# bf16 casts ahead of bf16 TensorE transposes, and DMA-cast MoE output weights, in a fused Longformer-attention and MoE kernel

## The chip, the cores and the metric

One core of one Trainium2 chip. Times are device microseconds (us) of that core; each run is one launch. In the views PE is TensorE and PEld its weight loads, DVE is VectorE, ACT ScalarE, POOL GpSimd and SP SyncE; a q after the name (SPq) is the engine's queue, which issues transfers. Those of SyncE go out on what the profile calls a hardware queue, those of GpSimd on a software queue; the core's 16 DMA engines carry both.

## The reference

```python
# q, k, v: [8 batches, 8 heads, 576 rows, 64]; global_idx: 8 sorted row numbers
scores = (1 / sqrt(64)) * q @ k.T
mask = (abs(i - j) <= 32) | i in global_idx | j in global_idx
attn = softmax(where(mask, scores, -1e9))
x = (attn @ v).transpose(0, 2, 1, 3).reshape(4608, 512)
h = x @ w_in                      # [512, 2048]
r = maximum(h, 0.0)
out = (s * r * r + b) @ w_out     # [2048, 512]; s and b are scalars
```

## The kernel before

A batch has four pairs of heads, a pair eight steps. Each step holds one block of scores, exponentials or products with v, and one "quantum" (a quarter of a row block) of the MoE of an earlier batch. Rows of q and k are cut in five blocks of 128, with 8 slots for the global rows in each (in q at row 60, in k and v at row 0). They are loaded as rows and transposed on TensorE; a transfer called the fill puts the global rows of a batch into their slots.

```python
natk = [const.tile([P, NCH, H, D], FP32, ...) for i in range(2)]   # natq the same
...
def load_q(eng, bi, h0, nh, part):          # 60 rows a block, two parts; load_k: 120 rows
    ...
    for c in range(NCH):
        a = KC * c + HB * part
        n = min(HB, S - a)
        r = (HB + NG) * part
        eng.dma_start(out=d[r : r + n, c, h0 : h0 + nh],
                      in_=q[bi, h0 : h0 + nh, a : a + n].rearrange("h s d -> s h d"))
...
def load_v(bi):                             # fp32 in DRAM, bf16 tile: cast by the DMA
    ... nc.gpsimd.dma_start(out=d[NG : NG + n, c, :, 0:D], in_=v[...])
...
def fill(bi):                               # the global rows of a batch, from DRAM scratch
    for d, src, r in ((natk[bi % 2], gsk, 0), (natq[bi % 2], gsq, HB), (vbufs[bi % 2], gsv, 0)):
        ... nc.sync.dma_start(...)
def prefetch_hw(bi):
    load_k(nc.sync, bi, 0, H)
    load_q(nc.sync, bi, 0, H, 0)
    load_q(nc.sync, bi, 0, H, 1)
    fill(bi)
...
def trans_a(p):                             # fp32 transposes, eviction casts to bf16
    ps = ps_s.tile([P, 512], FP32, tag="s", name="pst")
    for c in range(4):
        tr(ps, P * c, natk[bi % 2], c, hp)
    ...
    nc.scalar.copy(out=kt[:, 0:512], in_=ps[:])
...
for p in range(4, 4 * B):                   # the loop from batch 1 on
    ...
    if hp == 1 and bi + 1 < B:
        load_v(bi + 1)
        prefetch_hw(bi + 1)
    run_pair(p, nq, p + 1 < 4 * B)          # transposes of pair p + 1 at steps 5 and 6
```

The sum of the rows of `w_out`, which the bias needs, is added up on VectorE while ScalarE casts the weights (`weights_out`).

The softmax here doesn't subtract the row's maximum and nothing guards it: scores larger than these inputs give would overflow.

## Time and profile before

| | before |
|---|---|
| median of 3 runs | 438.07 us (436.57 to 438.22) |
| profiled span | 436.0 us |
| first score product of batches 0 to 7 | 20.2, 96.2, 124.0, 165.5, 207.0, 248.4, 289.8, 331.2 us |
| one batch, from batch 2 on | 41.4 to 41.5 us |
| PE busy over the whole span | 387.0 us |
| first MoE product | 72.7 us |

A batch's length is the distance between the first score products of two batches in the trace. The two things to keep in mind for what follows: from batch 2 on PE is the bound (busy 38.6 to 38.7 of every 40 us from 160 to 320 us), and k of the next batch is issued at 256.21 us but first read by a transpose at 285.08 us, 28.9 us later:

```profile
285.08 0.60 PE L349 MATMUL pst<-identf,natk 128*128 128x128 f32 x4
```

(The timeline of PE before: start, length, engine, line, operation, output from inputs.)

### The profile page before, as it was taken

Reading aid. Unit: us, or ns where it says so; the run is one execution under the profiler, and the core shown is the slowest. Engines: PE = TensorE matmul, PEld = TensorE weight load, DVE = VectorE, ACT = ScalarE, POOL = GpSimd, SP = SyncE. Lnnn points to the kernel's source line nnn. Section 1 sums busy time; section 2 is a strip of 40 time slices with the busy share of each in tenths; the row PEclk is TensorE's granted clock in tenths of the full one; section 3 lists DMA queues with packets and bytes.
Section 4 is the critical chain, followed back from the end, with each engine's and each line's share of the span. In section 5 each row is a group of like instructions: output and inputs, shape, how many; then the busy total and the mean of one; then the engine's idle time right before and its main releaser. Section 6 shows DMA issues by size and latency. Waiting matters only on the chain.

```text
span 436.0 us, 8254 instructions
## 1 busy us (share of the span) xinstructions
PE 387.0 (89%) x3063; PEld 241.8 (55%) x3063; DVE 265.6 (61%) x650; ACT 206.7 (47%) x405; POOL 84.5 (19%) x162
## 2 busy tenths in 40 slices
PE   1686984869799999999999999999999999999996
PEld 1563761325455655775577568656755665554442
DVE  7817443597776766676677567666766775442432
ACT  1013321855556733763476447645754673360530
POOL 9744932005005001300310050005000100100000
PEclk9999999989999999999999999999999999999999
DMA  8999194499519911991396169419941000101001
GB/s 134 154 229 257 13 147 58 170 193 97 55 48 151 150 46 67 157 143 52 88 147 111 50 122 148 75 57 138 140 86 50 26 0 30 71 2 65 31 26 72
DMA packets 128367, 42.00 MB, mean 96 GB/s; under 512 B 118655, under 2 KB 120703, under 8 KB 128327
## 3 DMA queue, kind: packets, MB, share of 16 engines
q1 hardware_dynamic: 83724, 34.00, 40.7%
q0 software_dynamic: 43328, 7.16, 24.1%
q8 instruction: 24, 0.39, 0.4%
q10 hardware_dynamic: 1275, 0.31, 0.4%
q14 instruction: 16, 0.13, 0.1%
HBM read 38.82 MB, written 9.83 MB: 112 GB/s over the span
## 4 chain that ended last, share of the span: by engine, by line
issue 49%; PE 30%; POOL 10%; ACT 5%; DVE 4%; POOLq 1%; DMA 1%; ACTq 0%; DVEq 0%
PE psh L518 10%; PE pso L533 10%; POOL vx L170 4%; POOL xt L498 3%; PE psg L391 3%; PE po L450 3%; PE pst L349 2%; ACT e L427 1%; ACT r L525 1%; PE pss L423 1%; DMA wo<-in_moe_w_out_dram 1%; POOL vx L124 1%; ACT kt L363 1%; POOLq L206 1%; DVE vx L417 1%
## 5 line engine op out<-in xcount | busy, mean ns | idle before, releaser
L518 PE MATMUL psh<-xt,win_t 128*128 128x512 bf16 (+7 forms) x1024 | 145.5, 289 | 15.8 <-POOL xt L498 12.3
L533 PE MATMUL pso<-wout_t,g 128*128 128x512 bf16 x576 | 141.1, 379 | 0.0
L525 ACT ACTIVATE r<-psh 128x512 bf16<-128x512 f32 x144 | 89.5, 627 | 80.7 <-PE psh L518 77.8
L427 ACT ACTIVATE e<-pss 128x384 bf16<-128x384 f32 (+1 forms) x160 | 75.5, 484 | 106.6 <-PE pss L423 105.4
L518 PEld LDWEIGHTS <-win_t 128*128 128x128 bf16 x1024 | 86.8, 98 | 62.6 <-issue 21.3
L528 DVE TENSOR_TENSOR g<-r 128x512 bf16<-128x512 bf16 x144 | 60.6, 424 | 53.8 <-ACT r L525 51.8
L533 PEld LDWEIGHTS <-g 128*128 128x128 bf16 x576 | 55.3, 98 | 55.9
L430 DVE TENSOR_TENSOR em<-e,mask 128x384 bf16<-128x384 bf16 (+1 forms) x160 | 54.6, 342 | 36.8 <-ACT e L427 35.5
L498 POOL COPY xt<-xg 128x4 bf16 x72 | 15.7, 218 | 271.9 <-DVE xg L496 239.1
L423 PE MATMUL pss<-qbd,kt 128*128 128x384 bf16 (+1 forms) x160 | 51.4, 337 | 12.1 <-POOL qbd L302 4.0
L542 DVE SCALAR_TENSOR_TENSOR osb<-pso,s_bc,bias_row 128x512 f32<-128x512 f32 x36 | 26.9, 747 | 31.8 <-PE pso L533 31.8
L381 DVE CAST qbd<-pst 64x512 bf16<-64x512 f32 x64 | 44.1, 689 | 2.1 <-PE pst L349 1.2
L450 PE MATMUL po<-em,vx 128*64 128x160 bf16 (+3 forms) x896 | 37.1, 233 | 3.1 <-DVE vx L417 1.7
L450 PEld LDWEIGHTS <-vx 128*64 128x64 bf16 x896 | 29.7, 117 | 14.5 <-issue 7.9
L349 PE MATMUL pst<-identf,natk 128*128 128x128 f32 x160 | 30.0, 295 | 8.7 <-DMA natk<-in_k_dram 8.6
L170 POOL DMA_DIRECT2D vx<-in_v_dram x40 | 35.3, 897 | 3.2 <-issue 3.2
L349 PE MATMUL pst<-identf,natq 128*128 128x128 f32 x160 | 28.8, 298 | 5.7 <-ACT kt L363 4.8
L349 PEld LDWEIGHTS pst<-identf,natk 128*128 128x128 f32 x160 | 20.9, 150 | 18.7 <-POOL identf masks.py:199 8.6
L481 DVE TENSOR_TENSOR xt<-po,rep 128x600 bf16<-128x600 f32 x32 | 25.1, 783 | 8.6 <-ACT rep L479 8.6
L423 PEld LDWEIGHTS <-kt 128*128 128x128 bf16 x160 | 15.5, 100 | 25.8 <-DVE qbd L381 6.1
L363 ACT CAST kt<-pst 128x512 bf16<-128x512 f32 x32 | 20.1, 629 | 18.2 <-PE pst L349 18.2
L349 PEld LDWEIGHTS pst<-identf,natq 128*128 128x128 f32 x160 | 19.7, 150 | 11.6 <-ACT kt L363 9.1
(75 smaller groups left out, 202.0 us busy)
## 6 DMA issues: line engine op xcount, KB each, us to landing
out_dram<-osb SPq DMA_DIRECT2D x36, 256.0 KB
natq<-in_q_dram SPq DMA_DIRECT2D x63, 120.0 KB
natk<-in_k_dram SPq DMA_DIRECT2D x28, 240.0 KB
wo<-in_moe_w_out_dram SPq DMA_DIRECT2D x4, 1024.0 KB
vx<-in_v_dram POOLq DMA_DIRECT2D x32, 120.0 KB, 8.4
win_t<-in_moe_w_in_dram POOLq DMA_DIRECT2D x4, 512.0 KB, 15.5
natk<-in_k_dram SPq DMA_DIRECT2D x7, 192.0 KB
natk<-in_k_dram SPq DMA_DIRECT2D x8, 120.0 KB
```

The lines of the kernel that those rows point to most:

```text
L170: nc.gpsimd.dma_start(out=d[NG : NG + n, c, :, 0:D], in_=v[bi, :, KC * c : KC * c + n].rearrange("h s d -> s h d"),)
L349: nc.tensor.transpose(ps[:, dst0 : dst0 + P], src2(src)[:, c, P * hp : P * hp + P], identf[:])
L381: nc.vector.tensor_copy(out=qdst(p, hh, 0, 512), in_=ps[r])
L423: nc.tensor.matmul(ps[:], ktile[p][:, P * c : P * c + P], qbufs[p % 3][:, :, LO[c] : HI[c]])
L427: nc.scalar.activation(e[:], ps[:], AF.Exp, scale=SCALE)
L430: later.append(lambda: nc.vector.tensor_mul(em[:], e[:], masks[c][:]))
L450: nc.tensor.matmul(po[D * hh : D * hh + D, a : a + n], vx[:, c, 2 * hp + hh, D * part : D * part + D], emt[(p, c)][:, hh, x : x + n], star ...
L498: nc.gpsimd.tensor_copy(out=xt[:, :, ds(greg_p[i], 1)], in_=xg[:, :, i : i + 1])
L518: nc.tensor.matmul(psh[:, d0 : d0 + n], win_t[:, a, f * P : f * P + P], xts[bi][:, a, x0 : x0 + n], start=(a == 0 and j == 0), stop=(a == ...
L525: nc.scalar.activation(r[:], psh[:], AF.Relu)
L528: later.append(lambda g=g, r=r: nc.vector.tensor_mul(g[:], r[:], r[:]))
L533: nc.tensor.matmul(pso[:], gl[f][:, u * P : u * P + P], wout_t[:, f], start=(f == 0), stop=(f == 15),)
```

## The change

Its intent: transposes in bf16 instead of fp32, twice as fast and evicted in fewer copies; `w_out` cast by the software queue's DMA instead of ScalarE, as `w_in` already was, and its row sum taken by accumulating transfers; the one-hot selection of global rows in the first two batches instead of the first alone, the rest taken from the DRAM scratch as before. To get bf16 rows, ScalarE casts k and q and GpSimd casts v, one batch ahead, from one fp32 tile for each. Core of the diff:

```diff
-    natk = [const.tile([P, NCH, H, D], FP32, ...) for i in range(2)]
-    natq = [const.tile([P, NCH, H, D], FP32, ...) for i in range(2)]
+    nat = {t: const.tile([P, NCH, H, D], FP32, ...) for t in "kqv"}
 ...
     def load_q(eng, bi, h0, nh, part):
         for c in range(NCH):
-            a = KC * c + HB * part
-            n = min(HB, S - a)
+            a = KC * c + (HB - NG) * part
+            n = min(HB + NG * part, S - a)          # the second part: 68 rows
 ...
-    def load_v(bi):                                  # GpSimd queue, casting
+    # load_kv(nc.gpsimd, "v", ...): GpSimd queue, fp32 to fp32; cast later by GpSimd
 ...
+    def cast(eng, t, bi, h0, nh):
+        hs = slice(h0, h0 + nh)
+        dst = vbufs[bi % 2][:, :, hs, 0:D] if t == "v" else cast_t[(t, bi)][:, :, hs]
+        eng(out=dst, in_=nat[t][:, :, hs])
 ...
-            nc.tensor.transpose(ps[...], src2(src)[:, c, ...], identf[:])      # fp32
+            nc.tensor.transpose(ps[...], src2(cast_t[(t, bi)])[:, c, ...], ident[:])  # bf16
 ...
+    def casts_for(bi):                               # third and fourth pair of a batch
+        return ({1: [cast k half 0 on ACT], 4: [cast q half 0 on ACT], 5: [cast v half 0 on POOL]},
+                {1: [cast k half 1 on ACT], 4: [cast q half 1 on ACT], 5: [cast v half 1 on POOL]})
+    def fetch(bi, fills):
+        load_batch(bi, 0, H)                         # k, q part 0, q part 1 on the sync queue
+        load_kv(nc.gpsimd, "v", bi, 0, H)
+        for t in fills:
+            fill(t, bi)
 ...
+    def wsum_part(j):                                # in batch 1: sum of w_out by DMA
+        if j == 0:
+            nc.sync.dma_start(out=wsum[:], in_=w_out2[:, 0:4])
+        else:
+            nc.gpsimd.dma_start(out=wsum[:], in_=w_out2[:, 4*j : 4*j+4], accum_op=OP.add)
 ...
         if hp == 1 and bi + 1 < B:
-            load_v(bi + 1)
-            prefetch_hw(bi + 1)
+            new_casts(bi + 1)
+            fetch(bi + 1, "kqv")
+        if hp >= 2 and bi + 1 < B:
+            ex = casts_for(bi + 1)[hp - 2]
```

(The bodies of `casts_for` are abbreviated here: each entry is a step of the pair and what is cast in it. The line `# load_kv ...` is a note and stands for code.)

## The prediction

> **What bounds the kernel now.** I read the engine table, the busy table by stretches of time, the groups by shape, the time line of one late batch, and the sync queue's time line, in that order.
>
> ```profile
> PE 387.0 (89%) x3063; PEld 241.8 (55%) x3063; DVE 265.6 (61%) x650; ACT 206.7 (47%) x405; POOL 84.5 (19%) x162
> ```
> ```profile
> 80.00:90.00 10.00, 6.57 (x30) 2.72 (x28) 7.11 (x15) 8.18 (x13) 0.00 (x0) 1.00 0.85 256
> ...
> 240.00:280.00 40.00, 38.67 (x358) 27.55 (x357) 27.74 (x69) 22.98 (x47) 6.01 (x13) 1.00 0.80 108
> ```
> ```profile
> L349 PE MATMUL pst<-identf,natk 128*128 128x128 f32 x160 | 30.0, 295 | 8.7 <-DMA natk<-in_k_dram 8.6
> L381 DVE CAST qbd<-pst 64x512 bf16<-64x512 f32 x64 | 44.1, 689 | 2.1 <-PE pst L349 1.2
> L378 DVE CAST qbd<-pst 64x128 bf16<-64x128 f32 x64 | 18.2, 284 | 0.4
> L391 PE MATMUL psg<-selq,natq 128*128 128x8 f32 x40 | 9.1, 361 | 0.0
> L600 ACT CAST wout_t<-wo 128x2048 bf16<-128x2048 f32 x4 | 7.6, 1905 | 0.3 <-DMA wo<-in_moe_w_out_dram 0.3
> ```
>
> The columns after a stretch are its length and the busy time of PE, PEld, DVE, ACT, POOL, then clock, DMA share, GB/s. From about 125 us on, PE is busy 38.7 of 40 us: it is the bound. Before that, waits bound: 80 to 90 us is 6.6 us of PE behind the output-weight casts.
>
> ```profile
> 256.46 0.20 POOL xt L498
> ...
> 297.86 0.21 POOL xt L498
> ```
> ```profile
> 265.86 0.14 PEld L349 LDWEIGHTS pst<-identf,natq 128*128 128x128 f32 x1
> ...
> 266.41 0.42 PEld L349 LDWEIGHTS pst<-identf,natq 128*128 128x128 f32 x4 [0.40 <-ACT kt L363]
> ...
> 266.80 0.86 PEld L518 LDWEIGHTS <-win_t 128*128 128x128 bf16 x8
> ```
> ```profile
> 256.21 4.32 SPq L150 DMA_DIRECT2D natk<-in_k_dram  x5
> 260.62 13.44 SPq L161 DMA_DIRECT2D natq<-in_q_dram  x10
> 274.10 0.47 SPq L324 DMA_DIRECT2D natk<-gsk  x1
> ```
>
> The chain of waits repeats every 41.4 us: one batch, four head pairs of eight steps, each step with a quarter of a MoE row block. In a pair the transposes take PE from 264.44 to 264.88 and from 265.75 to 266.80, 1.49 us, of which 0.4 wait for the ACT eviction. The sync queue needs 18 us to issue one batch of k and q loads; the global rows (the fill) come last, at 274.1, and stream until about 279 in the trace's packets. Nobody waits for that here: the tiles are double, and the first transpose of the batch comes later.
>
> [...]the trace has no bf16 transpose, its fp32 ones take 105 to 110 ns each in the run above. [...]From 256 to 279 us the trace's hardware queue has 247 four-byte semaphore packets, beside the 16 of one store: 60 and 120 rows on 15 engines, 96 on 16, 36 on 12, 8 on 8 (76+75+72+24=247).[...]
>
> **The change, part by part.** *Transposes:* ten at an estimated 56 ns are 0.56 us in place of 1.49, so 0.93 a pair, 3.7 a batch. The new block phase also hides the 1 us that the first product after POOL's row copies waits each batch. PE alone would need 41.4-4.7, about 37 us a batch, 1.16 a step.
>
> *DVE:* before, a pair has 2x689+2x284+283 = 2.2 us of evictions; after, three copies of 640 elements, 1.5 us at 2x or 2.5 at 1x. DVE has 27.7 of 40, so neither binds.
>
> *ACT:* loses 0.63 a pair (k eviction), gains four casts of 128x1280 a batch: at 1905/2048 = 0.93 ns an element 1.2 us each, 5 a batch. They fall in the third and fourth pair. The third has eight Relus (5.0), five Exps (2.4), Ln and reciprocal (1.5) and two casts (2.5): 11.4 us against PE's 9.3. Some 2 us a batch come back, even with data ready: 39.
>
> *Start:* fp32 selects cost 4.07 us a pair on the chain; in bf16, ten small matmuls are under 1 us. Three pairs after the first go from 11.4 to about 9, 6.5 and 6.5. DVE's added memsets and the first casts set the first score product at about 24 us instead of 20.2. First MoE product: 63 instead of 72.7. Block before batch 1: 14 quanta in 72.7 to 96.5 become 11 quanta and the first transposes in some 14 us, to 77; the ACT weight casts, the 1 MB waits and 11 DVE additions are gone. Batch 1 itself has more (casts, bf16 selects): about 31 us without waits, for 28.5.
>
> *Loads:* this is the step that decides. k, q and v now have one fp32 tile each. ACT's k cast for the next batch stands in step 1 of the third pair and reads all rows, the fill rows too. Loads can be issued at about step 4.7 of the first pair (after the store before them in the queue): call it T. The cast is due 12.3 steps plus 1 us later, T+15. Before, the fill landed at about T+20 (274.1-256.2 = 17.9 to its issue). After, it depends on q's second part: it has 68 rows instead of 60[...]. So four loads of 544 rows-times-heads of 256 B go over four engines, 136 packets each. On those engines, a batch is k 320, q first part 160, q second part 576, v 320: 1376 packets instead of some 900. One engine passed 50 to 57 packets/us in the 256 to 270 us stretch (1514 to 1831 packets in 2 us over 15 or 16 engines), 19 ns each: 26 us[...]: T+27 to T+28. ACT would wait about 12 us, in order, Exps and Relus behind it.
>
> PE runs on over two free score buffers and three MoE buffers, to step 4 of the third pair (23.2 us after the batch's start), then stops. ACT gets the rows at 33, casts, then works off its backlog: third pair over near 41.7, fourth near 51. **Period 51 us**, against 41.4. Batch 1 prefetches batch 2 in the same way with shorter pairs: about 13 us of wait. The last batch casts nothing: 38.
>
> Sum: batch 1 from 77 to 121 (31+13); five batches of 51 to 376; the last to 414; tail 62.6 as before plus two quanta 1.7, 478; the run's time stands 2 above the span (438.07 to 436.0): **480 us**.
>
> **Rivals.** (a) *The loads spread over all engines* (rounding up, or other engines for each transfer): the fill lands at T+20 as before. ACT waits 4 us, PE is set back to about 43 a batch, batch 1 waits 5: 113+215+38+64+2 = 432, about the same. For it: the trace does not show a 68-row transfer.[...] (b) *The fill is in time*, or ACT's wait disappears in PE's buffers: 108+5x39+38+64+2 = 407, 7% faster. For it: PE is truly the bound now and everything else in the change is a saving. Against: already before, fills land 20 us after the first load, and T+15 is too soon for that. (c) *Worse than my sum:* after each 12 us stop the PE clock falls (the stretch table gives 0.83 at 90 to 100 us after stops), and the accumulating weight-sum transfers hold POOL's queue ahead of batch 2's v casts: +10 to +20, 490 to 500.
>
> **Range and chances.** I give the four-engine case (with (c)) seven tenths, 480 to 500 less what a shorter queue would save, (a) two tenths, (b) one tenth. The middle comes to 474, a little under the sum because errors in T and the packet rate, multiplied by five batches, mostly lie on that side. Range 425 to 503. Faster by over 2%: 0.14; within 2%: 0.12; slower: 0.74.
>
> **What would show it.** Right: batches 50 us apart, ACT's cast of k in the third pair begins 10 us or more after the instruction ahead of it, released by the fill of the k rows (natk from gsk); PE idle 10 us in each third pair, behind ACT's Exp; DMA share low in the last third of each load; transposes near 56 ns; first MoE product near 63. Wrong: batches at 37 to 40 us, casts that start at once, or q loads landing within 20 us of T. I am wrong most if 68 rows spread over more than four engines.

Its estimates from before any run, beside what the traces show: a bf16 transpose 56 ns, and 56 from start to start in the trace after (L357, median from 50 us on; the 256-column bf16 matmuls of the kernel before, L518, start 109 ns apart); an eviction of 640 elements "at 2x", which is half the 1.05 ns an element of the fp32 copies before (284 ns for 128 elements, 689 for 512), and 485 ns after; ten selects under 1 us, and 0.45 us after (from 21.00 us); loads of 68 rows over four engines, of which the kernel before has none and which the trace after shows by 4 semaphore updates each (under the experiments). That the four are the same in every load, as the 1376 packets take it, no trace shows.

## The result, and the profile after

| | before | after |
|---|---|---|
| median, same chip | 437.34 us (436.57 to 438.22, 4 runs) | 503.18 us (501.51 to 504.97, 4 runs) |
| ratio | 1 | 1.1505, 95% interval 1.1456 to 1.1555 |
| span, mean granted clock of the profiled run | 436.0 us | 501.5 us, 0.908 |

A ratio here and below is the mean time of one kernel's runs over that of the kernel before's runs of the same rounds, so not quite the ratio of the medians. The kernel is 15% slower, at the upper edge of the predicted range, 0.2 us above it.

The engine table after: PE has 23 us less work, and yet its share falls from 89 to 73%.

```profile
PE 364.3 (73%) x3063; PEld 216.1 (43%) x3063; DVE 248.4 (50%) x604; ACT 219.9 (44%) x401; POOL 99.3 (20%) x173
```

Groups after (line, engine, operation, output from inputs, count | busy us, mean ns | idle before them and what ended it). The savings came: the eviction of 640 elements takes 485 ns, the select 173 ns instead of 361, and casts of 1260 ns were added. The idle time before the casts is the new thing.

```profile
L377 DVE COPY qbd<-pst 64x640 bf16<-64x640 bf16 x64 | 31.0, 485 | 0.6
L204 ACT CAST ck<-natk 128x1280 bf16<-128x1280 f32 x15 | 18.9, 1260 | 70.1 <-DMA natk<-gsk 56.5 <-issue 13.7
L677 POOL DMA_DIRECT2D wsum<-in_moe_w_out_dram x3 | 3.9, 1294 | 41.6 <-DMA wsum<-in_moe_w_out_dram 41.6
```

The batches now start at 22.9, 78.9, 124.1, 181.8, 235.2, 289.2, 344.2 and 398.3 us: their lengths are 56.0, 45.2, 57.7, 53.4, 54.0, 55.1 and 54.1, where the kernel before had 41.4 from batch 2 on. Stretches after (length, then busy us of PE, PEld, DVE, ACT, POOL, granted clock, DMA share, GB/s): ten us in the middle of a stop, one whole batch, and the last batch, which prepares no next one.

```profile
210.00:220.00 10.00, 0.83 (x5) 0.55 (x5) 1.10 (x3) 3.02 (x6) 0.00 (x0) 0.50 0.37 87
235.20:289.20 54.00, 39.58 (x366) 26.33 (x365) 26.24 (x62) 26.09 (x48) 8.74 (x15) 0.87 0.49 94
398.30:436.00 37.70, 37.70 (x360) 23.31 (x359) 24.21 (x61) 22.97 (x46) 1.63 (x8) 1.00 0.08 29
```

PE works 39.6 of 54.0 us, and 37.7 of 37.7 in the last batch. So the batch itself did become shorter (last batch against last batch, its final product with v starts 34.9 us into it where it was 38.4), and something that belongs to the next batch's preparation costs 16. The sync queue's timeline after, for batch 4's loads, shows the long issue of q (20.3 us where it was 13.44):

```profile
188.27 4.14 SPq L153 DMA_DIRECT2D natk<-in_k_dram  x5
192.51 20.30 SPq L162 DMA_DIRECT2D natq<-in_q_dram  x10
212.84 0.41 SPq L335 DMA_DIRECT2D natk<-gsk  x1
```

And ScalarE's timeline after, 4.1 us later, where the square bracket is the idle time before the instruction and what ended it:

```profile
216.98 1.26 ACT L204 CAST ck<-natk 128x1280 bf16<-128x1280 f32 x1 [13.71 <-DMA natk<-gsk]
```

The cast of k stood ready in ScalarE's queue at 203.3 us and waited for the fill, 28.7 us after the load's first issue. Behind it, in order, stood the exponentials and Relus that TensorE needs: 210 to 220 us is nearly empty on every engine.

Batch 2 is different. Its cast of k doesn't wait: the loads that it needs were issued at 119.92 us, the cast runs at 164.26 with no idle time before it. Its stop comes from the sum of `w_out`, first a plain load of 1 MB (109.73 us), then three accumulating ones (start, length, what in the chain), and below them the two waits of TensorE that it ends in:

```profile
109.73 6.25 DMA wsum<-in_moe_w_out_dram
116.53 9.33 DMA wsum<-in_moe_w_out_dram
...
136.52 13.00 DMA wsum<-in_moe_w_out_dram
```

```profile
139.09 1.81 PE L446 MATMUL po<-em,vx 128*64 128x160 bf16 x28 [7.50 <-POOL vx L204]
...
151.79 2.04 PE L685 MATMUL psb<-wsum,onesf 128*128 128x512 f32 x2 [5.27 <-DVE wsum L683]
```

The three accumulating transfers wait for each other in GpSimd's queue (for the plain one 24.3 us, then 8.5 and 8.8). The casts of v stand behind them and start at 137.27 us, so TensorE waits 7.5 us for v; then the bias product waits 5.3 us for the sum itself.

### The profile page after: what moved, and what is told of

The parts are those of the page before. It is cut to its first block, busy times and chain, and to the rows that moved or that the text cites. A ratio compares the mean times of both kernels' runs of the same rounds, so it can differ in the third digit from the quotient of the medians.

```text
span 501.5 us, 8207 instructions
## 1 busy us (share of the span) xinstructions
PE 364.3 (73%) x3063; PEld 216.1 (43%) x3063; DVE 248.4 (50%) x604; ACT 219.9 (44%) x401; POOL 99.3 (20%) x173
## 3 DMA queue, kind: packets, MB, share of 16 engines
q0 software_dynamic: 9776, 17.71, 19.2%
## 4 chain that ended last, share of the span: by engine, by line
PE 48%; SPq 16%; issue 14%; DMA 11%; POOL 4%; ACT 4%; DVE 2%; POOLq 0%; ACTq 0%
PE pso L531 22%; PE psh L516 17%; SPq L162 16%; DMA wsum<-in_moe_w_out_dram 6%; PE po L446 3%; PE pss L419 3%; DMA natk<-gsk 2%; PE pst L357 2%; ACT r L523 2%; DMA natv<-in_v_dram 2%; ACT e L423 1%; DMA natq<-in_q_dram 1%; POOL natv L153 1%; POOL wout_t L641 1%; POOL gsv L327 1%
## 5 line engine op out<-in xcount | busy, mean ns | idle before, releaser
L516 PE MATMUL psh<-xt,win_t 128*128 128x512 bf16 (+7 forms) x1024 | 154.0, 301 | 5.0 <-POOL xt L494 5.0
L426 DVE TENSOR_TENSOR em<-e,mask 128x384 bf16<-128x384 bf16 (+1 forms) x160 | 60.8, 381 | 50.6 <-ACT e L423 49.5
L204 POOL CAST vx<-natv 128x1280 bf16<-128x1280 f32 x16 | 21.6, 1404 | 143.9 <-DMA natv<-gsv 136.1
L204 ACT CAST ck<-natk 128x1280 bf16<-128x1280 f32 x15 | 18.9, 1260 | 70.1 <-DMA natk<-gsk 56.5
L545 DVE SCALAR_TENSOR_TENSOR osb<-pso,s_bc,bias_row 128x512 f32<-128x512 f32 x32 | 23.9, 747 | 42.3 <-PE pso L531 42.3
L153 POOL DMA_DIRECT2D natv<-in_v_dram x40 | 36.7, 928 | 1.2 <-issue 1.0
L357 PEld LDWEIGHTS <-ck 128*128 128x128 bf16 x160 | 13.3, 110 | 49.2 <-issue 24.9
L357 PE MATMUL pst<-ident,ck 128*128 128x128 bf16 x160 | 16.6, 244 | 23.5 <-DVE ck L204 20.0
L377 DVE COPY qbd<-pst 64x640 bf16<-64x640 bf16 x64 | 31.0, 485 | 0.6
L204 ACT CAST cq<-natq 128x1280 bf16<-128x1280 f32 (+1 forms) x17 | 20.7, 1220 | 17.6 <-DVE gadd L305 14.0
L419 PEld LDWEIGHTS <-kt 128*128 128x128 bf16 x160 | 15.5, 101 | 22.9 <-DVE qbd L398 7.9
```

The source lines that it names most:

```text
L153: eng.dma_start(out=nat[t][r : r + n, c, h0 : h0 + nh], in_=src[t][bi, h0 : h0 + nh, a : a + n].rearrange("h s d -> s h d"),)
L204: eng(out=dst, in_=nat[t][:, :, hs])
L357: nc.tensor.transpose(ps[:, P * c : P * c + P], src2(cast_t[(t, bi)])[:, c, P * hp : P * hp + P], ident[:],)
L419: nc.tensor.matmul(ps[:], ktile[p][:, P * c : P * c + P], qbufs[p % 3][:, :, LO[c] : HI[c]])
L426: later.append(lambda: nc.vector.tensor_mul(em[:], e[:], masks[c][:]))
L516: nc.tensor.matmul(psh[:, d0 : d0 + n], win_t[:, a, f * P : f * P + P], xts[bi][:, a, x0 : x0 + n], start=(a == 0 and j == 0), stop=(a == ...
```

## The experiments

The theory after the result: the cast made the loads due 15 us after their issue, where the transposes before read them 28.9 us after it; what makes the loads take 28 us is (1) the second part of q, whose 68 rows go over four DMA engines, and perhaps (2) v's transfers on the same engines. Rivals: the single fp32 tile, the place of the fill at the end of the queue, and the bias's transfers.

That 68 rows go over four engines is in the trace as a count. It has the semaphore updates with which each transfer lands: 16 for a store, 16 for a load of 128 rows, 15 for one of 120 or 60, 13 for 104, 11 for 44, and 4 for each load of 68, besides one near the issue where they are fewer than 16 (the third load of 68, issued at 207.03 us, lands with those of 212.33, 212.36, 212.52 and 212.94 us). I read the number as that of the engines at work; which engines they are, the records do not say. The four-byte packets agree: from 188.2 to 225 us the hardware queue has 234, and 32 for two stores, 76 for k, 75 for the first part of q, 27 for the second (4 for each of four loads, 11 for the fifth) and 24 for three fills are 234. Rounding rows up over 16 engines would leave more: 248 in place of the 202 of the loads and fills. From 208 to 212 us, when the 68-row loads run, the mean busy share of the 16 engines is 0.31; from 190 to 192 us, in k's loads, it is 1.25 (records of packets overlap).

All kernels below gave correct results.

**a1_q64: each 68-row load split in 64 and 4 rows.**

```diff
-            eng.dma_start(out=nat["q"][HB*part : HB*part + n, ...], in_=q[..., a : a + n] ...)
+            for o, m in ((0, 64), (64, n - 64)) if n > 64 else ((0, n),):
+                r = HB * part + o
+                eng.dma_start(out=nat["q"][r : r + m, ...], in_=q[..., a + o : a + o + m] ...)
```

> One edit to the changed kernel: each 68-row load of q's second part is issued as 64 rows and 4 rows, so that the large part divides by 16. If the loads on four engines hold up the fill of the k rows (my theory), the fill is issued some 17 us after the first k load instead of 24.6 and lands near 20 instead of 28.7; ACT's wait before the first k cast of a batch falls from 13.7 us to about 5, the batch from 54 us to about 45, the run to 445 to 460 us. If the single fp32 tile or the order of the queue is the cause, the loads cost the same bytes and the time stays within 2% of 503.

Measured: 481.04 us (478.55 to 483.42), ratio 1.0977 (1.0923 to 1.103). Batches 3 to 6 take 50.7 to 51.6 us. ScalarE's timeline:

```profile
206.28 1.26 ACT L206 CAST ck<-natk 128x1280 bf16<-128x1280 f32 x1 [11.32 <-DMA natq<-in_q_dram]
```

Load issued at 179.95, cast at 206.28: 26.3 us instead of 28.7. The four engines are a real cost, but only about 3 of the 13 us by which a batch is too long.

**a2_fill_early: the fill of k issued right after k's loads, ahead of q.**

```diff
     def fetch(bi, fills):
-        load_batch(bi, 0, H)
+        load_kv(nc.sync, "k", bi, 0, H)
+        fill("k", bi)
+        load_q(nc.sync, bi, 0, H, 0)
+        load_q(nc.sync, bi, 0, H, 1)
 ...                                   # the other fills stay where they were
```

> One edit: the fill of the k rows is issued right after the k loads, ahead of the q loads. Theory of the four engines: the k cast no longer waits, but q's cast, three steps later, then waits for q's own fill behind the same loads, until 29 to 32 us after the first load, so a batch keeps 50 us or more and the run 485 to 500 us. Rival, that only the fill's place at the end of the queue costs: both casts find their rows, 430 to 445 us.

Measured: 509.2 us (508.37 to 511.68), ratio 1.1647 (1.1586 to 1.1708). The waits before k's cast fall to 0.1 to 3.8 us, and q's cast takes them over. Waits (engine, line, what was waited for: us in all, times, longest):

```profile
ACT cq L204 <- DMA natq<-gsq: 38.2, 3, 15.8
...
ACT cq L204 <- DMA out_dram<-osb: 10.3, 1, 10.3
ACT cq L204 <- DMA natv<-gsv: 10.1, 1, 10.1
```

The order in the queue only chooses which cast waits. A gain of a few us was expected; it came out slightly slower.

**a3_two_tiles: two fp32 tiles for k and q and one bf16 tile instead of the reverse; loads in the same place.**

```diff
-    nat = {t: const.tile(...) for t in "kqv"}
+    nats = {(t, i): const.tile(...) for t, i in (("k",0),("k",1),("q",0),("q",1),("v",0))}
-    castp = ... tc.tile_pool(name="castp", bufs=2)
+    castp = ... tc.tile_pool(name="castp", bufs=1)
```

> Two fp32 tiles each for k and q in turn (as the kernel before has), with one bf16 cast tile in place of two to make room; the loads stay where they are in the sync queue. My theory: the loads start at the same point, since the store ahead of them in the queue and not the free tile sets it, so within 1.5% of 503. Rival, that the single tile makes the loads late: a clear fall, to 470 or less.

Measured: 503.1 us (500.58 to 503.51), ratio 1.1481 (1.1425 to 1.1536), waits of 13.5 to 14.6 us. So a second tile alone gains nothing. Whether a single tile could be loaded as early as the next run does was not tried.

**a4_early_fetch: a3, and the loads and fills of k and q two pairs of heads earlier.**

```diff
-            fetch(bi + 1, "kqv")          # second pair of batch bi
+            fetch(bi + 1, "v")
+        if hp == 3 and bi + 2 < B:        # fourth pair of batch bi, for the batch after next
+            fetch(bi + 2, "kq")
```

> As the two-tile run, and the k and q loads with their fills are issued two pairs earlier (68-row loads unchanged, v where it was). My theory: the loads still take 25 us or more, but the casts come 30 us and more after them, so ACT's waits before the casts go; batches 3 to 6 take 38 to 41 us and the run about 425 to 435, with the wait for the weight sums in batch 2 left. Rival, that ACT's added work (5 us of casts a batch in front of Relus and Exps) sets the time: batches stay at 45 us or more, 460 to 500.

Measured: 441.73 us (439.95 to 442.89), ratio 1.0106 (1.0062 to 1.015). Batches 3 to 6 take 38.9 to 39.0 us and no cast of k waits in them. One of these batches, in the stretches:

```profile
218.30:257.10 38.80, 37.37 (x362) 24.97 (x364) 25.45 (x62) 25.85 (x48) 8.59 (x15) 1.00 0.63 133
```

PE is busy 37.4 of 38.8 us, at full clock. With the same four-engine loads, 61 of the 66 us are gone. The run changes two things, though: v's loads stay where they were, so k and q no longer run beside them and all their packets have started after 20.6 to 22.4 us instead of 26.7 to 28.5. But the cast now comes 40.3 to 41.3 us after the load's issue, more than the slow loads needed too. That the distance alone would do is an inference from these numbers, and not what the run shows by itself. The time itself lies above the 425 to 435 that was expected, because batches 1 and 2 (43.9 and 57.8 us) kept their waits.

**a5_bias_pe: the row sum of w_out by TensorE from the bf16 weights, no transfers for it.**

```diff
-        nc.tensor.matmul(ps[:], onesf[:], wsum[:, 0])
+        for f in range(16):
+            nc.tensor.matmul(ps[:], onesb[:], wout_t[:, f], start=(f == 0), stop=(f == 15))
```

(and `wsum_part` and the additions are taken out)

> The changed kernel with the weight sums of the bias taken by TensorE from the bf16 weights in SBUF (16 products with a tile of ones) in place of one load and three accumulating transfers of 1 MB each and the additions: the whole of the disputed cost taken away. In the changed kernel batch 2 takes 57.7 us, the others 54. If the wait for the sums merely takes the place of the wait for the fill in that batch, this run gains 3 to 8 us (495 to 500); if the sums are a cost of their own on top, 15 us or more (under 490).

Measured: 492.87 us (490.59 to 494.38), ratio 1.1263 (1.1204 to 1.1321). Batch 2 falls from 57.7 to 44.1 us, batch 3 grows from 53.4 to 56.0: about 10 us in all, between the two outcomes that were expected. The trace decides: batch 2 had no wait for the fill that the sums could have hidden (0.0 us before its k cast in both kernels). So the bias's transfers are a second, separate cost, of 13.6 us in that batch and 10 in all.

**a7_v_late and a8_q64_v_late: v's loads written one pair later from batch 2 on, alone and with a1's split.**

```diff
-            fetch(bi + 1, "kqv")
+            fetch(bi + 1, "kqv" if bi == 1 else "kq")
+        if hp == 2 and 1 < bi and bi + 1 < B:
+            fetch(bi + 1, "v")
```

(GpSimd's casts of v are moved later to match, into steps 5 and 6 of the fourth pair.)

> The changed kernel with v loaded one pair later from batch 2 on (68-row loads kept), so that v's 4096-byte packets of the software queue no longer run beside the k and q loads. Theory that v's large packets crowd out k and q on the DMA engines for some 8 us: the fill of k lands about 20 to 22 us after the first load instead of 28.7, batches 3 to 6 take 45 to 48 us, the run 467 to 480. Rival, that the four-engine loads alone set it: fill at 27 us or later, 495 to 505.

> Both: 64-row and 4-row loads, and v one pair later. If the two causes add (2.4 us by the first as measured, some 7 by the second), the fill lands 17 to 19 us after the first load, ACT waits 2 to 3 us, batches 3 to 6 take 41 to 44 us and the run 440 to 452. If a third cause holds the fill back[...], batches stay at 47 us or more.

Measured: 506.79 us (504.92 to 508.43, ratio 1.1598) and 483.46 us (482.7 to 485.79, ratio 1.1071), within 1% of the kernels without the edit. As tests these failed: GpSimd runs ahead in its own queue, so v's loads were still issued 2.6 us after the first load of k (192.30 and 189.71 us), as in the changed kernel (190.87 and 188.27). They say nothing of v.

**a6_all: a1, a3, a4 and a5 together.**

> Early loads into two tiles of k and q each, 64-row loads, and the bias from the bf16 weights, together. Theory: the change's savings are real and only its waits hide them; batch 2 falls from 57.8 to about 40, batch 1 from 43.9 to 33 to 38, batches 3 to 6 stay at 39: 403 to 418 us, faster than the kernel before. Rival, that the savings were never there: at 437 or above.

Measured: 423.21 us (421.39 to 423.89), ratio 0.9672 (0.9627 to 0.9717): faster than the kernel before, though above the 403 to 418 expected. Batch 2 is down to 44.5 us and batches 3 to 6 stay at 39.0; one cast in batch 1 still waits. In the waits:

```profile
ACT ck L214 <- DMA natk<-gsk: 7.2, 1, 7.2
```

**a10_v_sync: the changed kernel with v's loads on the sync queue, behind the fills of k and q.**

```diff
         load_batch(bi, 0, H)
-        load_kv(nc.gpsimd, "v", bi, 0, H)
-        for t in fills:
-            fill(t, bi)
+        fill("k", bi)
+        fill("q", bi)
+        load_kv(nc.sync, "v", bi, 0, H)
+        fill("v", bi)
```

> The changed kernel with one edit: from batch 2 on, v's loads go to the sync queue, behind the fills of k and q, in place of GpSimd's software queue; the 68-row q loads, over four engines, stay. Theory (v's 4096-byte packets take the engines for some 8 us just when k and q's 256-byte packets should pass): the fill of k lands about 19 us after the issue instead of 28.7, the wait before k's first cast falls from 13.7 us to about 5, batches 3 to 6 last 44 to 46 us, and the time is 460 to 472. Rival (the four-engine loads alone set the fill, or the order of a queue does, and v's packets only fill gaps): batches stay at 53 to 55 and the time at 500 or more.

Measured: 480.56 us (478.24 to 481.97), ratio 1.0981 (1.0926 to 1.1035). Batches 3 to 6 take 47.5 to 48.2 us. Two views of it, the sync queue's timeline and ScalarE's:

```profile
191.64 4.63 SPq L153 DMA_DIRECT2D natk<-in_k_dram  x5
196.37 14.10 SPq L162 DMA_DIRECT2D natq<-in_q_dram  x10
210.52 0.50 SPq L335 DMA_DIRECT2D natk<-gsk  x1
```

```profile
214.41 1.26 ACT L204 CAST ck<-natk 128x1280 bf16<-128x1280 f32 x1 [7.77 <-issue]
```

The cast starts 22.8 us after the first issue instead of 28.7; the four-engine loads are still there. So v's transfers beside k and q are the larger of the two costs. The edit changes more than their time: v also leaves GpSimd and its software queue, where one batch of it is 304 packets of 4096 bytes, which a12 below takes up in part. The time missed its 460 to 472: the wait that is left is 7.4 to 8.6 us and not 5, and batch 2 became longer (65.5 us instead of 57.7), where TensorE's longest wait for v's cast, behind the bias's transfers in GpSimd's queue, is 18.8 us; it was 7.5 in the changed kernel.

**a11_q64_v_sync: a1 and a10 together.**

> The same edit together with the q loads split into 64 and 4 rows. Theory (the two costs, four engines for q and v's large packets, make up the whole wait between them): the fill of k lands 14 to 16 us after the issue, no wait or at most 1 us before k's first cast, batches 3 to 6 of 39 to 41 us, and the time 425 to 440, with only batch 2's wait for the bias's transfers left. Rival (a third cause, such as the fill's place behind all of q): batches of 47 or more and a time above 465.

Measured: 453.22 us (451.29 to 454.68), ratio 1.0384 (1.0339 to 1.0429). Batches 3 to 6 take 43.3, 41.3, 43.0 and 42.0 us, batch 2 64.6. ScalarE's timeline:

```profile
243.19 1.26 ACT L206 CAST ck<-natk 128x1280 bf16<-128x1280 f32 x1 [2.29 <-DMA natk<-gsk]
```

The cast starts 17.3 us after the load's issue (225.86). The two costs together explain all but 2 to 4 us of the wait. The 425 to 440 was missed, by 7 us of batch 2 and by these waits in five batches.

**a12_q64_v_cast: a1, with v of batches 2 on cast by the DMA into the bf16 tile, as before the change.**

```diff
-        load_kv(nc.gpsimd, "v", bi, 0, H)                     # fp32 to fp32
+        nc.gpsimd.dma_start(out=vbufs[bi % 2][r : r + n, c, :, 0:D], in_=v[...])   # casting, 5 times
+        nc.gpsimd.dma_start(out=vbufs[bi % 2][0:NG, c, :, 0:D], in_=gsc["v"][bi])  # the fill, 5 times
```

(and GpSimd's casts of v are taken out)

> The kernel with the q loads split into 64 and 4 rows (a1_q64: 481.04 us, batches of 50.7 to 51.6), with v of batches 2 on loaded as in the kernel before: cast to bf16 on its way by the software queue, its fill too, and no casts of v on GpSimd. In the trace of the kernel before, v of one batch is 4608 packets of 128 bytes, whose times add up to 9.7 us on each of the 16 engines; in the changed kernel it is 304 packets of 4096 bytes, 6.4 us on each. Theory A (the harm is in the size: a 4096-byte packet holds up the 256-byte packets queued at its engine[...]): the fill of k is issued about 18 us after the load as before, k's first cast waits 5 to 6 us, batches 3 to 6 last 46 to 47, the time is 455 to 465. Theory B (the harm is v's time on the engines, whatever its packets): the fill is issued 22 us or later after the load, the wait stays at 10 us or more, batches last 51 or more, the time is 480 or more.

It asks whether the size of v's packets is what harms; in the changed kernel's trace one batch of v is 304 packets of 4096 bytes. Measured: 475.82 us (472.83 to 477.11), ratio 1.088 (1.085 to 1.091). Batches 3 to 6 take 48.1 to 49.9 us. Its sync queue and ScalarE:

```profile
177.63 5.62 SPq L153 DMA_DIRECT2D natk<-in_k_dram  x5
183.36 15.34 SPq L164 DMA_DIRECT2D natq<-in_q_dram  x14
198.74 0.37 SPq L337 DMA_DIRECT2D natk<-gsk  x1
```

```profile
202.24 1.26 ACT L206 CAST ck<-natk 128x1280 bf16<-128x1280 f32 x1 [9.61 <-DMA natk<-gsk]
```

The fill is issued after 21.1 us (20.2 and 20.5 in the next two batches): between the 18 of theory A and the 22 of theory B, nearer to B. Two of 51 us come back. So the packet's size is a small part of what v costs; that v's transfers run at the same time is most of it: a11, with v behind, is 8.8 us below a1's batch. Theory B's reading, by the time that v's packets take, isn't confirmed either: in a12's own trace v and its fill are 5184 packets whose times add up to 16.7 us on each engine, more than the 6.4 of the plain load, and yet the wait is shorter. Records of packets overlap (from 183.6 to 185.6 us they fill the 16 engines' time 3.4 times), so such sums don't measure what v takes from k and q.

**The transfers side by side.** From the trace's DMA records: when half, three quarters and all of the 256-byte packets of k and q of one batch had started, in us from the load's first issue (my count, 9216 packets before and 9792 in the others), beside the wait before k's cast and the mean of batches 3 to 6:

```
kernel           50%    75%   100%   wait before k's cast   batch
before          11.1   16.0   21.8   (no cast)               41.4
after           11.7   18.5   27.3   13.7 to 15.2            54.15
a1 (q split)    11.8   19.2   24.5    9.8 to 11.3            51.15
a12 (+ v cast)  11.7   17.5   23.1    8.4 to  9.6            49.15
a10 (v behind)   7.9   12.1   21.6    7.4 to  8.6            47.8
a11 (both)       8.1   11.7   17.5    2.3 to  3.8            42.4
a4 (earlier)     8.2   12.7   22.4   none                    39.0
```

Each row is one batch; batches of one kernel differ by some 3 us in a column at most (after: 10.5 to 13.7, 18.1 to 19.2, 26.7 to 28.5; before: 11.1 to 12.7, 16.0 to 17.0, 20.9 to 22.4). The middle columns show the two costs apart. With v behind, half of k and q is through by 8 us instead of 11.7; that is v's share of the engines. The last quarter takes 8.8 us in the changed kernel and 9.5 in a10, and 5.3 to 5.8 where q is split; that is the four engines. Alone the split gains 3.0 us a batch and the move of v 6.4, together 11.8: each hides part of the other.

The 8 us in which v is densest show it too. In the 8 us from 194 to 202 us of the changed kernel, 289 packets of 4096 bytes of v pass and only 380 KB of k and q; in the 8 us from 260 to 268 of the kernel before, with v in packets of 128 bytes, 713 KB of k and q do. In a12, from 184 to 192 us, it is 476 KB.

These windows make the plain load look worse than it is, because v starts later after k's load in the changed kernel. Counted over the first 14 us from the load's issue, in batches 3 to 6, k and q start 5309 to 5672 packets before, 4951 to 5608 after, 5672 to 6218 in a12, and 7721 to 7927 in a10. So v held k and q back nearly as much in the kernel before. There the first reader came 28.9 us after the issue, and nobody waited; the change did not create this cost, it made it count.

**a9_all_castmove: a6, with the k and q casts moved from the third and fourth pair to the fourth and the next batch's first, which have no Relu.**

```diff
-            {1: [cast k half 0], 4: [cast q half 0], 5: [cast v half 0]},
-            {1: [cast k half 1], 4: [cast q half 1], 5: [cast v half 1]},
+            {5: [cast v half 0]},
+            {1: [cast k half 0], 3: [cast q half 0], 5: [cast v half 1]},
 ...
-        if bi == 1 and hp == 0:
-            ex = {1: [cast k half 1 of batch 1], 4: [cast q half 1 of batch 1]}
+        if hp == 0:
+            ex = {1: [cast k half 1 of batch bi], 4: [cast q half 1 of batch bi]}
```

> The version that beat both kernels, with the k and q casts of ScalarE moved out of the third pair of heads, which holds the Relu of the MoE, to the fourth pair and the next batch's first. Theory (the casts cost their batch 1.3 us, the 39.0 of a middle batch over the 37.7 of the last one, because they share a pair with the Relu): 414 to 418. Rival (those 1.3 us belong to the loads and to the work of a next batch as a whole, not to the pair that the casts lie in): the same as without the move, 421 to 424.

Measured: 410.08 us (409.73 to 411.76, 6 runs), ratio 0.9393 (0.9362 to 0.9425): 6.1% faster than the kernel before, the best of all. PE is busy 86% of the span. One batch in the stretches:

```profile
189.40:227.30 37.90, 37.39 (x363) 25.03 (x365) 26.15 (x62) 25.82 (x48) 8.79 (x15) 1.00 0.66 137
```

Not for the reason written, though. Batches 3 to 6 went from 39.0 to 37.8, 37.9, 38.4 and 38.6 us: 0.4 to 1.2 us each, 3.3 in all, instead of 1.3 each. Of the 14.0 us between the two spans 8.2 come from batch 1 (38.8 to 30.6 us), whose cast was due before its loads had landed and now isn't, and 1.8 from batch 2.

## Why the prediction was right or wrong

**The direction was right, and so was the mechanism outside batch 2.** ScalarE's k cast waits 13.7 us ("about 12", "10 us or more"), is released by the fill of the k rows, and TensorE stands still behind ScalarE. Transposes start 56 ns apart in the last batch (five of them at 404.51 to 404.74 us), the first MoE product comes at 64.0 us (63), batch 1 starts at 78.9 (77), batch 2 at 124.1 (121), and the last batch takes about 38 us (38; its end is not sharp in the trace). The evictions run at the 2x that the prediction left open: 640 elements in 485 ns, 1.5 us for three as it had for that case. That is 0.53 ns an element above the 149 ns that the 284 and 689 ns of the fp32 copies leave for none, against 1.05 ns before (estimates from these times).

**The size failed.** The step that failed is the term "Period 51 us", and then the weighting: "The middle comes to 474, a little under the sum because errors in T and the packet rate, multiplied by five batches, mostly lie on that side." No line works 474 out, and the errors lay on the other side. The sum's span of 478 us was 501.5:

| term | predicted | measured | difference |
|---|---|---|---|
| start of batch 1 | 77 | 78.9 | +1.9 |
| batch 1 | 44 | 45.2 | +1.2 |
| batch 2 | 51 | 57.7 | +6.7 |
| batches 3 to 6, each | 51 | 53.4, 54.0, 55.1, 54.1 | +12.6 in all |
| last batch and tail | 38 + 64.3 | 103.2 | +0.9 |

In batches 3 to 6 "ACT gets the rows at 33" was 35.2, 35.2, 36.7 and 35.2 us: the loads were issued 6.4 to 6.5 us into the batch and not 5.5 (4.7 steps of 1.16), and the cast began 28.7 to 30.3 us after them and not 27 to 28. From there to the next batch it took 18.2 to 18.9 us, predicted 18.

In batch 2 the mechanism was wrong, and that the 51 missed by no more than 6.7 us was luck. The wait for the fill that it contains did not come (0.0 us); the bias's transfers stood in its place, as rival (c) had them, holding up v's casts. a5 took them away and the batch fell by 13.6 us. Rival (c)'s 490 to 500 was nearest; its clock term is there too (0.50 in the stop, 0.87 over the batch), but a stop's clock was not tested apart from the stop.

**The load step gave nearly the right landing time from a wrong model.** It puts the whole rise from "some 900" to 1376 packets on q's second part, over four engines. By its own 19 ns, spreading that part over 16 would save 418 packets or 7.9 us (an estimate from its numbers); a1 brought the cast only 2.4 us nearer, and with v out of the way 5.5 (22.8 us in a10, 17.3 in a11). v it counts as 320 packets an engine, 6.1 us; the trace has 304 packets of 4096 bytes for the whole batch, 336 ns each on average, 6.4 us on each engine. So that time was right from wrong packets, and a10 brought the cast 5.9 us nearer. The four-engine stretch runs at some 14.5 ns a packet and engine and not 19 (545 and 554 packets in 2 us over four engines, from 208 to 212 us). The count behind the 19 mixes packets of 256, 128 and 4 bytes; from 258 to 270 us I count 1514 to 1909 in 2 us. That these errors offset one another in the landing time was luck.

**Rival (a) was right in no part.** With the loads on all engines it put the fill at T+20 and the time at 432; a1 has the cast at T+26.3 and 481.

**Rival (b)'s arithmetic was right, its premise wrong.** It put a batch with its loads in time at 39; a4 shows 38.9 to 39.0. The change's savings are real; the waits for the fill and for the bias hid them.

**What stays open.** Small packets of v (a12) still leave k and q slower than in the kernel before, and the lag arises when most of v has passed: between 14 and 20 us after the issue 3269 to 3674 packets start before, 2685 to 3066 in a12. Why, and which part of the wait of 2.3 to 3.8 us in a11 belongs to the fill's latency, no run tells.

## What to carry to other kernels

Putting a cast ahead of a consumer moves the moment at which the load is due (here from 28.9 us after its issue to 15): compute the distance from issue to first reader before and after, not only the cost of the cast. A wait in an in-order engine that also serves the bound engine can cost its whole length in every period: here waits of 13.7 to 15.2 us stood in batches of 54.15 us, and batches without them (a4) took 39.0. Look at what a transfer shares the engines with (moving v behind k and q gained 6.4 us a batch), and at how many engines its rows go over (splitting the loads that went over four gained 3.0), before blaming its own bytes; and when a tuned schedule gets slower, move the loads before giving up the change: here the same change went from 15% slower to 6% faster, with the earlier loads, the split of q, the bias on TensorE and the moved casts together.

## What the runs measured of the transfers

- A software-queue load beside hardware-queue loads: k and q started 7721 to 7927 packets in the first 14 us when v came after them (a10), 4951 to 5608 beside a plain load of v and 5309 to 5672 beside a casting one, and moving v behind them saved 6.4 us of a 54 us batch.
- A cast and how a software-queue load is cut: one batch of v was 4608 packets of 128 bytes with the cast and 304 of 4096 bytes without.
- The number of engines and the rate: 68 rows went over four (4 semaphore updates for each such load). There a 256-byte packet took some 14.5 ns on each of the four, and about 17 to 18 ns where 15 or 16 engines worked (1784 packets in the 2 us from 190 us of the changed kernel).
- A chain of accumulating software-queue transfers: three of 1 MB each, one after the other, held GpSimd for 8.5 and 8.8 us between their issues, and the last took 13.0 us in the chain.
